# Splitting the output-weight load of a decode-attention kernel into 120 and 8 partitions

## The chip, the core and the metric

The kernel runs on one core of a Trainium2 chip. The metric is the device time of one execution in microseconds (us). Before the change the median of three runs is 2008.08 us (2006.43 to 2009.18).

## What is computed

Two independent attention blocks, A and B, decode one token each for a batch of two. Per block: 32 heads of 192, a cache of 8192 keys and values per head and batch entry, a model width of 640, everything in bf16. The two results are put side by side.

```python
q = (x @ wq).reshape(B, Sq, Hq, Dh).transpose(0, 2, 1, 3)      # B=2, Sq=1, D=640, Hq=32, Dh=192
scores = jnp.einsum("bhqd,bhkd->bhqk", q, k) * (Dh ** -0.5)    # k, v: (2, 32, 8192, 192)
p = _softmax(scores, axis=-1)
o = jnp.einsum("bhqk,bhkd->bhqd", p, v)
return o.transpose(0, 2, 1, 3).reshape(B, Sq, Hq * Dh) @ wo    # wo: (6144, 640)
# both blocks: jnp.concatenate([a, b], axis=-1)
```

Each key and value is used once, so the kernel is above all a stream of some 837 MB out of device memory.

## The kernel before

**Units.** The work is cut into 128 units, numbered `u`: block, then head, then batch entry. Head number `g` is `u // 2`. Each unit loads one 3 MB slab of keys (`kb`) and one of values (`vb`), laid out as 128 partitions by 64 rows by 192, so that each partition receives one run of 24576 bytes. There are two buffers for each.

**Engines.** VectorE multiplies the keys by the query, which stands broadcast over the partitions (L247 and L251), and sums a part of the products (L258, L262); ScalarE sums the other part (L269) and does the exponentials (L276); GpSimd does the maximum and the sum over partitions (L234, L238); TensorE multiplies the probabilities by the values (L344, 64 matmuls per unit). At the end of each pair of heads TensorE turns the result (L352) and multiplies it by the output weight (L379, called `f5` in the code, six matmuls), summing a block's result in `outps`.

**Weights.** Both weights are loaded in groups of four heads, numbered `w` from 0 to 15, with two buffers each: `wqs` (960 KB) and `wos` (960 KB). A load of `wos` has 128 partitions, and each partition receives two runs of 3840 bytes (three rows of the output weight for each of two head pairs).

**Order of the loads.** All loads are issued by SyncE (SP), one after the other, from one list written out by hand: keys of unit 0, keys of 1, values of 0, keys of 2, values of 1 and so on. `sp_wo(w)` stands behind the keys of unit `8w + 1`, ahead of the values of the unit before. A load waits until its buffer is free: keys for the multiply of two units ago (`d1b`), values for the matmuls of two units ago (`pv`), the output weight for the `f5` that last used its buffer. A DMA raises its semaphore by 16 when it has landed, and `reg` holds, for each name, the semaphore and the value that a reader waits for. Only the results (L320 of the code, `out_dram`, two rows of 640 bytes each) are stored from ScalarE's own queue.

**Who waits for the output weight.** `f5` of head pair `pp` waits for `("wo", (2 * pp) // HG)`. Waits are merged by `_Stream.emit`: an engine that has already waited for a value does not wait again, so there is one such wait on TensorE in each group, at the first `f5` that uses it.

## Time and profile before

| | |
|---|---|
| median of the runs | 2008.08 us (2006.43 to 2009.18) |
| profiled execution, first to last instruction (the span) | 2005.8 us |
| busy: TensorE, VectorE, ScalarE, GpSimd | 56%, 74%, 72%, 7% of the span |
| DMA packets | 55986, 838.05 MB, 418 GB/s in the mean |
| the load queue's packets | 98.8% of what 16 DMA engines have in the span |
| `wos` loads | 16 of 960 KB, 25.1 us from issue to landing (median) |

The profile gives the span of the one execution that was traced; it is 2.3 us below the median of the runs, which is what lies around the first and the last instruction and the scatter between executions. The page's DMA rows are means over 16 engines. A "landing" is the last of the 16 steps by which a load's semaphore rises. The trace also holds the time of every such step and of every DMA packet (start, duration, size, queue), but not the number of the engine that moved it.

### The profile page before, as it was taken

Reading aid. Unit: us, or ns where it says so; the run is one execution under the profiler, and the core shown is the slowest. Engines: PE = TensorE matmul, PEld = TensorE weight load, DVE = VectorE, ACT = ScalarE, POOL = GpSimd, SP = SyncE. Lnnn points to the kernel's source line nnn. Section 1 sums busy time; section 2 is a strip of 40 time slices with the busy share of each in tenths; the row PEclk is TensorE's granted clock in tenths of the full one; section 3 lists DMA queues with packets and bytes.
Section 4 is the critical chain, followed back from the end, with each engine's and each line's share of the span. In section 5 each row is a group of like instructions: output and inputs, shape, how many; then the busy total and the mean of one; then the engine's idle time right before and its main releaser. Section 6 shows DMA issues by size and latency. Waiting matters only on the chain.

```text
span 2005.8 us, 19822 instructions
## 1 busy us (share of the span) xinstructions
PE 1116.4 (56%) x5014; PEld 592.4 (30%) x5014; DVE 1484.8 (74%) x962; ACT 1435.5 (72%) x7811; POOL 143.6 (7%) x270
## 2 busy tenths in 40 slices
PE   2565555556555565556654565546655565555557
PEld 1232323223232233223322333223332233222323
DVE  7777877877777777777777767777677776877676
ACT  6776777767767676776767767777677776777776
POOL 2000100000000001000000000000000020000001
PEclk9776777777777777777777777777777777777778
DMA  9999999999999999999999999999999999999995
GB/s 389 429 428 431 430 429 431 429 431 427 428 426 426 423 413 430 419 425 420 420 430 407 424 420 418 429 411 428 416 417 433 413 423 422 410 433 414 430 417 235
DMA packets 55986, 838.05 MB, mean 418 GB/s; under 512 B 7352, under 2 KB 18240, under 8 KB 22848
## 3 DMA queue, kind: packets, MB, share of 16 engines
q1 hardware_dynamic: 55856, 836.79, 98.8%
q8 instruction: 39, 0.64, 0.1%
q14 instruction: 75, 0.61, 0.1%
q10 hardware_dynamic: 16, 0.01, 0.0%
HBM read 836.77 MB, written 0.01 MB: 417 GB/s over the span
## 4 chain that ended last, share of the span: by engine, by line
DMA 74%; PE 20%; DVE 4%; ACT 2%; issue 0%; POOL 0%; SPq 0%
DMA vb<-in_A_v_cache_dram 38%; DMA vb<-in_B_v_cache_dram 22%; PE ops L344 19%; DMA kb<-in_B_k_cache_dram 13%; DVE prodD L251 2%; DVE prodA L247 2%; ACT prodA L269 1%; DMA kb<-in_A_k_cache_dram 1%; POOL mg L234 0%; PE outps L379 0%; PE oTps L363 0%; PE oTps L352 0%; SPq L187 0%; SPq L194 0%; ACT pb L276 0%
## 5 line engine op out<-in xcount | busy, mean ns | idle before, releaser
L344 PE MATMUL ops<-vb,pb 128*33 128x384 bf16 x4096 | 954.1, 408 | 880.1 <-DMA vb<-in_A_v_cache_dram 451.2
L269 ACT ACTIVATE prodA<-prodA 128x192 bf16<-128x192 bf16 x3582 | 1239.7, 351 | 238.3 <-DVE prodA L247 238.2
L344 PEld LDWEIGHTS ops<-vb,pb 128*33 128x33 bf16 x4096 | 481.9, 120 | 1352.8 <-issue 1207.4
L269 ACT ACTIVATION_READ_ACCUMULATOR prodA<-prodA 128x1 f32 x3582 | 680.7, 190 | 0.0
L247 DVE TENSOR_TENSOR prodA<-kb,qbc 128x5376 bf16<-128x5376 bf16 x128 | 378.5, 2957 | 281.4 <-DMA kb<-in_A_k_cache_dram 142.5
L251 DVE TENSOR_TENSOR prodD<-kb,qbc 128x6912 bf16<-128x6912 bf16 x128 | 480.4, 3753 | 1.2 <-DMA kb<-in_A_k_cache_dram 1.2
L258 DVE TENSOR_TENSOR prodD<-prodD 128x3456 bf16<-128x3456 bf16 (+2 forms) x384 | 464.8, 1210 | 13.3
L254 DVE TENSOR_REDUCE mp<-sc 128x1 f32<-128x64 f32 x128 | 28.2, 220 | 201.4 <-ACT prodA L269 201.3
L234 POOL PARTITION_ALL_REDUCE mg<-mp x128 | 50.2, 392 | 1734.0 <-DVE mp L254 1734.0
L262 DVE TENSOR_REDUCE sc<-prodD 128x36 f32<-128x864 bf16 x128 | 134.8, 1053 | 4.4
L283 ACT ACTIVATE o_sb<-ops 1x384 f32<-1x384 f32 x63 | 30.3, 480 | 123.8 <-PE oTps L352 95.7
L311 ACT ACTIVATE qbc<-qps 128x384 bf16<-128x384 f32 x64 | 31.4, 491 | 92.5 <-PE qps L332 92.5
L273 ACT ACTIVATE nb<-mg 128x1 f32<-128x1 f32 x128 | 26.0, 203 | 99.5 <-POOL mg L234 99.5
L238 POOL PARTITION_ALL_REDUCE lall<-rs x128 | 85.8, 670 | 103.0 <-ACT pb L276 103.0
L352 PEld LDWEIGHTS oTps<-ones,o_sb 33*128 33x128 f32 x372 | 67.1, 257 | 9.8 <-issue 9.8
L352 PE MATMUL oTps<-ones,o_sb 33*128 33x1 f32 x372 | 69.8, 311 | 0.0
L276 ACT ACTIVATE pb<-sc,nb 128x64 bf16<-128x64 f32 x128 | 52.2, 408 | 4.3 <-ACT nb L273 0.2
L332 PE MATMUL qps<-wqs,xbc_0 128*128 128x384 bf16 x160 | 32.5, 335 | 6.1 <-DMA wqs<-in_A_wq_dram 6.1
L332 PE MATMUL qps<-wqs,xbc_1 128*128 128x384 bf16 x160 | 32.4, 334 | 0.6 <-ACT qbc L311 0.6
L379 PE MATMUL outps<-wos,oTz 128*4 128x320 bf16 x192 | 32.1, 304 | 0.1
L284 ACT ACTIVATE o_sb<-ops 1x384 f32<-1x384 f32 x63 | 30.4, 482 | 0.7
L276 ACT ACTIVATION_READ_ACCUMULATOR pb<-sc,nb 128x1 f32 x128 | 23.9, 187 | 0.0
(30 smaller groups left out, 84.8 us busy)
## 6 DMA issues: line engine op xcount, KB each, us to landing
vb<-in_A_v_cache_dram SPq DMA_DIRECT2D x64, 3072.0 KB, 23.0
kb<-in_A_k_cache_dram SPq DMA_DIRECT2D x63, 3072.0 KB, 24.0
kb<-in_B_k_cache_dram SPq DMA_DIRECT2D x63, 3072.0 KB, 23.8
vb<-in_B_v_cache_dram SPq DMA_DIRECT2D x62, 3072.0 KB, 23.2
wos<-in_A_wo_dram SPq DMA_DIRECT2D x8, 960.0 KB, 25.1
wqs<-in_B_wq_dram SPq DMA_DIRECT2D x8, 960.0 KB, 27.5
wos<-in_B_wo_dram SPq DMA_DIRECT2D x8, 960.0 KB, 25.1
wqs<-in_A_wq_dram SPq DMA_DIRECT2D x7, 960.0 KB, 27.5
```

The source lines that it names most:

```text
L234: return lambda eng: eng.partition_all_reduce(mg[u % 2][:], mp[u % 2][:], 128, bass.bass_isa.ReduceOp.max)
L238: return lambda eng: eng.partition_all_reduce(lall[g % 2][:, b:b + 1], rs[u % 2][:], 128, bass.bass_isa.ReduceOp.add)
L247: return lambda eng: eng.tensor_tensor(prodA[u % 2][:, 0:na, :], kb[u % NK][:, 0:na, :], qb_bc(u, na), ALU.mult)
L251: return lambda eng: eng.tensor_tensor(prodD[:, 0:T - na, :], kb[u % NK][:, na:T, :], qb_bc(u, T - na), ALU.mult)
L258: return lambda eng: eng.tensor_tensor(prodD[:, 0:nd, 0:w], prodD[:, 0:nd, 0:w], prodD[:, 0:nd, w:2 * w], ALU.add)
L262: return lambda eng: eng.tensor_reduce(sc[u % 2][:, na:T], prodD[:, 0:T - na, 0:24], AXL.X, ALU.add)
L269: return lambda eng: eng.activation(prodA[u % 2][:, t, :], prodA[u % 2][:, t, :], ACTF.Identity, accum_out=sc[u % 2][:, t:t + 1])
L276: return lambda eng: eng.activation(pb[u % 2][:, :, ::32], sc[u % 2][:].rearrange("p (j a) -> p j a", a=2), ACTF.Exp, bias=nb[u % 2][:], s ...
L332: ins = eng.matmul(qps[:, 0:QW], xbc[blk][b][:, c, :], wqs[w % 2][:, c, off:off + QW], start=(c == 0), stop=(c == DC - 1))
L344: ins = eng.matmul(ops[(u // B) % 2][0:33, b, 0:QW], pb[u % 2][:, j, :], vv[:, j, :], start=(j == 0), stop=(j == T // 2 - 1))
L352: ins = eng.matmul(oTps[:, 2 * i + b:2 * i + b + 1], o_sb[:, b, :, :].rearrange("p s (r i) -> p i (s r)", i=3)[:, i, :], ones33[:], start= ...
L379: ins = eng.matmul(outps[0:4, 0:NH2], oTz[pp % 2][:, i, 2 - 2 * half:6 - 2 * half], wos[w % 2][:, pr, i, half * NH2:(half + 1) * NH2], sta ...
```

## The change

Each load of `wos` is issued as two loads, one straight after the other: partitions 0 to 119 with the semaphore that was there, and partitions 120 to 127 with a new one (`wohsem`). `f5` waits for both. Sizes, order, buffers and all arithmetic stay as they are; SP issues 313 rows in place of 297.

```diff
+        wohsem = [sem(f"wohsem{i}") for i in range(2)]
...
             reg[("wo", w)] = (wosem[w % 2], 16 * (w // 2 + 1))
+            reg[("woh", w)] = (wohsem[w % 2], 16 * (w // 2 + 1))
...
-        def sp_wo(w):
+        WP = 120
+
+        def sp_wo(w, part):
             blk = (w * HG) // Hn
             h0 = (w * HG) % Hn
             src = blocks[blk]["wo"][h0 * Dh:(h0 + HG) * Dh, :].rearrange("(pr p i) n -> p pr (i n)", p=128, i=3)
-            return dma(wos[w % 2][:].rearrange("p pr i n -> p pr (i n)"), src, wosem[w % 2])
+            dst = wos[w % 2][:].rearrange("p pr i n -> p pr (i n)")
+            if part == 0:
+                return dma(dst[0:WP], src[0:WP], wosem[w % 2])
+            return dma(dst[WP:128], src[WP:128], wohsem[w % 2])
...
-            w = [("f4", pp), ("wo", (2 * pp) // HG), key("f5", pp - 1)]
+            w = [("f4", pp), ("wo", (2 * pp) // HG), ("woh", (2 * pp) // HG), key("f5", pp - 1)]
...
-                    S_sp.add(sp_wo(w), waits=[key("f5", ((w - 2) * HG + HG - 1) // 2 if w >= 2 else -1)])
+                    S_sp.add(sp_wo(w, 0), waits=[key("f5", ((w - 2) * HG + HG - 1) // 2 if w >= 2 else -1)])
+                    S_sp.add(sp_wo(w, 1))
```

## The prediction

> **What bounds the kernel now.** I read the page's sections 2 to 4 first, then the waits, the stages, and the tile `wos`.

> ```profile
> GB/s 389 429 428 431 430 429 431 429 431 427 428 426 426 423 413 430 419 425 420 420 430 407 424 420 418 429 411 428 416 417 433 413 423 422 410 433 414 430 417 235
> ...
> q1 hardware_dynamic: 55856, 836.79, 98.8%
> q8 instruction: 39, 0.64, 0.1%
> q14 instruction: 75, 0.61, 0.1%
> q10 hardware_dynamic: 16, 0.01, 0.0%
> ...
> DMA 74%; PE 20%; DVE 4%; ACT 2%; issue 0%; POOL 0%; SPq 0%
> ```

> The loads (q1) fill 98.8% of the mean DMA engine; 74% of the chain that ended last is DMA. No compute engine is over 74% busy. The waits, over all engines and then SP's own:

> ```profile
> PE ops L344 <- DMA vb<-in_A_v_cache_dram: 451.2, 64, 22.9
> PE ops L344 <- DMA vb<-in_B_v_cache_dram: 427.5, 64, 10.5
> ...
> SPq L187 <- PE ops L344: 1086.3, 126, 13.3
> SPq L187 <- DVE prodD L251: 777.8, 126, 12.0
> ```

> TensorE waits for values; SP waits for free buffers, its loads already queued. Two stages of the windows view (columns: length, then busy and count of PE, PEld, DVE, ACT, POOL, the clock, the DMA share, GB/s):

> ```profile
> 100.00:600.00 500.00, 282.97 (x1266) 150.18 (x1264) 371.33 (x242) 358.83 (x1956) 33.62 (x66) 0.73 1.01 429
> 600.00:1080.00 480.00, 269.60 (x1204) 143.42 (x1205) 358.34 (x232) 346.56 (x1889) 31.46 (x61) 0.73 1.00 422
> ```

> The same work runs at 429 GB/s up to 600 us and at 422 after, at one clock. The reason is in the 16 steps of each load's semaphore, one per DMA engine. From the trace's records, in us after the first step of the load:

> ```
> load ends at   2nd   8th   14th  15th  16th step
>  47 us (v)     0.03  0.15  0.35  0.36   0.84
> 207 us (k)     0.01  0.19  1.82  1.94   4.33
> 411 us (v)     0.03  1.67  2.03  2.25   9.17
> 571 us (k)     0.01  1.78  3.49  3.60  13.47
> 1317 us (k)    0.06  0.68  1.43  1.90  13.88
> ```

> **One DMA engine, call it X, falls behind all others** until it is some 13.5 us late. Then the two-deep buffers stop the rest, which is the fall to 422 GB/s. X never stops. Its landings between 23 and 1992 us add to 1981.2 us, against 1938.8 for its packets at their usual durations (a 24576-byte packet starts 912 ns after the one before). 64 of the 291 intervals are over 300 ns too long, by 46.9 us together; 62 of the 64 hold a q14 instruction packet. Such a packet of 8192 bytes sits in X's own sequence (309 ns, and the next takes some 380 ns longer: about 0.69 us). So X carries an instruction stream (by its even pace that of ScalarE with its 7811 instructions) besides its sixteenth of the loads, and X's sum is the kernel's time. The q8 packets fall on changing engines.

> **Which engine X is.** The stores of the result (q10) have two partitions each:

> ```profile
> out_dram<-out_sb ACTq DMA_DIRECT2D x4, 1.2 KB
> ```

> Their semaphore shows three steps per store, one at the issue and two later: two engines. At 1082.97 us one of the 640-byte packets starts where a packet of X ends, and at 1084.85 a q14 packet starts where the next of these ends. X is one of the two engines that even a two-partition DMA uses; both stores used the same two.

> **The change, part by part.** The old `wos` loads:

> ```profile
> L187 SPq DMA_DIRECT2D wos<-in_A_wo_dram x8: 435/436/2255, 11.3 to 870.2; - x8
> L187 SPq DMA_DIRECT2D wos<-in_B_wo_dram x8: 431/435/449, 993.8 to 1866.0; - x8
> ...
> DMA to landing us min/median/max: 14.3/25.1/25.3
> ```

> 1. Removed: 16 loads of 128 partitions. Each gives X 8 partitions, 16 packets of 3840 bytes; X spends 2.28 us on a load (mean of 16), so 142 ns a packet.

> 2. Added: 16 loads of 120 partitions. 128 went to 16 engines in equal parts and 2 to two, so I take 120 as 15 times 8, with X among the 15, since X is in the smallest set: 16 packets on X as before, no change in their number.

> 3. Added: 16 loads of 8 partitions, on 8 engines, X among them: two more packets on X per load, 2 x 0.142 = 0.285 us, and one more completion packet (they start 6 ns apart): 0.29 us, times 16 = **4.7 us**. X has no idle time, so all of it is on the path. The engine that is left out of the 15 saves 2.28 us per load, which buys nothing, as it already waits for X.

> [...]

> 4. Unknown: what a packet of such a split costs. Every load in this trace has 128 partitions, so each partition's bytes always came through one engine, and each engine ran alone at one rate (24576 bytes in 912 ns, 3840 in 142). With 15 engines that assignment has to shift, and X writes, at least for some partitions, where another engine writes all the time; others write where X does. If only the engine sets the pace, nothing is added: 4.7 us is the low end. If the destination does, two streams share it. Nearest row for that: from 1083 to 1088 us, as the results are stored and the stopped engines start again, packets of 24576 bytes take 1.0 to 2.1 us in place of 0.91, up to 2.3 times. At twice, X's 18 packets cost 18 x 2 x 0.142 - 2.28 = 2.85 us more per load, times 16 = **45.6 us**. If the others' packets also hold up X's keys and values for as long as a load's packets last, 2.28 more per load: 82 us, the high end. Below nothing this part has no way, as no packet here is faster than 912 ns or 142 ns.

> I take the middle, 45.6 us: the rate is the same to the nanosecond in all engines and for large and small packets, which looks like a fixed width that one stream fills; and I count only one of the two directions.

> [...]

> 5. SP issues 16 more DMAs, at the 0.44 us of the row above or less: 7 us on a queue that waited for buffers for 1864 us. Behind them stand the values of the unit before, issued some 15 us or more before they land. Without that cover they would cost 0.4 us per load. Nothing on the path.

> 6. TensorE waits 16 more times, before the first `f5` of a group. `wos` is issued at 248.3 us for a group whose `f5` is about five units of 15.7 us later; it lands after 25. Behind that wait are the next matmuls of L344, which wait for values anyway. Nothing, unless the load took over 70 us.

> Sum: 2005.8 + 45.6 = 2051.4 us of span; with the 2.3 us between span and median, **2053.7 us**.

> **The rivals.**

> - **Only the two packets count**: +4.7, 2012.8 us. For it: 4.7 is what the packet durations give alone, and they never vary with size. Against it: no row has two engines in one place. It is slower by just over 0.2%, which is about what a measurement of this kernel can tell from no change.
> - **X is the engine left out (faster).** If 120 partitions go to a set of 15 without X and the 8 to a set without it too, X saves 2.28 x 16 = 36.5 us. The next engine then sets the time. X's lag behind the 15th engine grew from 0.46 us at 23 us to 9.97 at 577.5, 17.2 ns per us, so 34 over the run; less 4.7 for the added packets: -29, 1979 us. It decides as soon as X's share falls by over 4.7 us in all. Against it: X carries packets of the two-partition stores, and a set of 15 without X next to a set of two with it would be odd. For it: the saving almost equals X's surplus.
> - **X's share stays** (8 of 120, none of the 8, no sharing of places): 2008.1 us.
> - **Fewer engines than 15**: if 120 goes in eights or less to a smaller set, X gets 15 or more partitions, at least 8 x 2 x 0.142 x 16 = +36 us, 2045 us, and over 2090 with sharing.

> **How the numbers follow.** Chances: places shared, with anything from +10 to +85 us, 0.55; two packets only, 0.22; X left out, 0.12; X's share unchanged, 0.05; fewer engines, 0.06. The range 2008 to 2090 holds the first two, the unchanged case and most of the last; below it lies X left out, above it a rest of 0.04. Faster by over 0.2%: 0.12. Within 0.2%: the unchanged case and a quarter of the two-packet one, whose 4.7 us is near the bound of 4.0: 0.10. Slower: 0.78.

> **What would show it.** X's time on a `wos` load (2.28 us between its landings) becomes about 2.57 if only packets count, and 4 to 7 us if places are shared; then also the durations of 3840-byte packets go from 149 ns towards 300, and packets of 24576 bytes near `wos` grow too. GB/s in the stage after 600 us falls below 422. One of the load's semaphores shows one early step (16 less 15), the other eight. I am wrong if X's lag shrinks and all engines land together (X left out), or if the wos packets still take 149 ns and the time rises by under 10 us.

## The result and the profile after

The changed kernel takes 2116.32 us (median of 4 runs, 2111.96 to 2117.5); the kernel before, in 4 runs, takes 2008.63. The ratio is 1.0536 (95% interval 1.0521 to 1.0551): slower by 107.7 us, where 45.6 were forecast, and above the end of the range, 2090.

The traced execution has a span of 2114.1 us, 108.3 more than before. First its page (sections 2 to 4):

```profile
GB/s 363 429 386 426 431 388 428 389 418 414 386 397 379 416 411 391 398 385 407 415 387 398 382 414 409 385 406 380 406 405 393 399 385 414 399 404 393 385 405 253
DMA packets 56099, 838.06 MB, mean 396 GB/s; under 512 B 7464, under 2 KB 18352, under 8 KB 22960
...
q1 hardware_dynamic: 55968, 836.79, 98.3%
...
DMA 78%; DVE 20%; ACT 1%; PE 0%; issue 0%; POOL 0%; SPq 0%
```

The same bytes, the DMA engines as full as before (98.3%), but 396 GB/s in place of 418. The row GB/s has holes of 379 to 390 all along; before, no slice between the first and the last was under 407. So packets are not waiting to be issued, they take longer. The q1 line has 112 packets more than before: 16 loads times (15 + 8 - 16) completion packets, so the two new loads use 15 and 8 engines; their semaphores show one early step and then 15 and 8 later ones.

The windows view, a stretch without and three with the first split load (columns: length, busy and count of PE, PEld, DVE, ACT, POOL, the clock, the DMA share, GB/s):

```profile
140.00:146.00 6.00, 2.40 (x8) 1.19 (x9) 5.90 (x4) 6.00 (x36) 0.00 (x0) 0.69 1.02 438
147.00:150.00 3.00, 3.00 (x13) 1.54 (x12) 0.83 (x2) 2.24 (x14) 0.35 (x1) 0.65 1.01 197
150.00:153.00 3.00, 1.64 (x11) 0.78 (x8) 0.00 (x0) 1.30 (x4) 0.39 (x1) 1.00 1.10 200
153.00:156.00 3.00, 0.00 (x0) 0.00 (x0) 0.57 (x1) 0.00 (x0) 0.00 (x0) 0.99 1.10 235
```

While `wos` is loaded, the DMA share is 1.01 to 1.10 and the core moves 197 to 235 GB/s, about half of the 438 before it. In the kernel before, with `wos` loaded among the keys and values in the same way, it ran at 425 and 451:

```profile
265.00:268.00 3.00, 3.00 (x13) 1.55 (x12) 2.90 (x4) 3.00 (x19) 0.00 (x0) 0.62 1.03 425
268.00:272.00 4.00, 2.96 (x19) 1.57 (x16) 1.03 (x3) 2.97 (x13) 0.74 (x2) 1.00 1.06 451
```

The tile `wos` (durations in ns, first and last start in us):

```profile
L189 SPq DMA_DIRECT2D wos<-in_A_wo_dram x16: 340/432/2327, 11.5 to 916.5; - x16
L189 SPq DMA_DIRECT2D wos<-in_B_wo_dram x16: 340/405/474, 1046.7 to 1968.6; - x16
...
DMA to landing us min/median/max: 17.9/31.8/32.8
```

`wos` lands 31.8 us after its issue (25.1 before). The waits (total us, times, longest), of all engines and then of SP's queue:

```profile
PE ops L351 <- DMA vb<-in_A_v_cache_dram: 507.3, 64, 26.9
PE ops L351 <- DMA vb<-in_B_v_cache_dram: 477.2, 63, 13.1
```

```profile
SPq L189 <- PE ops L351: 1182.1, 126, 15.0
SPq L189 <- DVE prodD L258: 784.3, 126, 13.2
```

The same waits as before are longer, none is new, and SP still waits for buffers. By size, from the trace's packet records (median ns of one): 3840 bytes, 149 before and 292 after; 24576 bytes, 912 in both, but 956 in the mean after and 925 before.

**Where the time went on X.** X, the engine that lands last in every load, never stops, so its landings can be laid end to end. Two kinds of interval changed. First, the one that holds `wos` (from the keys before it to the values after it), above the values' own 7.30 us. Second, the two loads just ahead of `wos`, above their own times: X is late (6.5 us behind the next engine at the third load, 9 to 13 us from the fifth on) and still writes these keys and values while the other engines already write `wos`. Means of 16, in us, with X's instruction packets in them in every kernel alike:

```
                          holds wos    two ahead    more per load, x 16     measured
before                       2.50         0.34               -                 -
after (120 + 8)              4.77         4.68      2.27 + 4.34 = 106        107.7
```

X pays 2.27 us as a guest, where its own `wos` packets go slowly, and 4.34 us as a host, where others' packets hold up its keys. In the load issued at 258.9 us its eight key packets, usually 912 ns, take 1199, 1634, 1813, 2533, 1640, 1016, 995 and 920; its 18 `wos` packets then take, in order:

```
149 149 149 169 302 314 314 314 304 301 185 171 284 301 301 300 | 286 296
```

(the last two are those of the 8-partition load). The other loads from the third on that could be followed packet by packet show the pattern of these 18 within some 40 ns a packet.

### The profile page after: what moved, and what is told of

The parts are those of the page before. It is cut to its first block, busy times and chain, and to the rows that moved or that the text cites. A ratio compares the mean times of both kernels' runs of the same rounds, so it can differ in the third digit from the quotient of the medians.

```text
span 2114.1 us, 19853 instructions
## 1 busy us (share of the span) xinstructions
PE 1119.0 (53%) x5014; PEld 592.8 (28%) x5014; DVE 1484.6 (70%) x962; ACT 1434.6 (68%) x7811; POOL 143.3 (7%) x270
## 3 DMA queue, kind: packets, MB, share of 16 engines
q1 hardware_dynamic: 55968, 836.79, 98.3%
## 4 chain that ended last, share of the span: by engine, by line
DMA 78%; DVE 20%; ACT 1%; PE 0%; issue 0%; POOL 0%; SPq 0%
DMA kb<-in_B_k_cache_dram 40%; DMA kb<-in_A_k_cache_dram 39%; DVE prodD L258 11%; DVE prodA L254 9%; ACT prodA L276 1%; PE ops L351 0%; POOL mg L241 0%; PE oTps L370 0%; PE outps L386 0%; SPq L189 0%; SPq L196 0%; ACT pb L283 0%; DVE mp L261 0%; ACT out_sb L322 0%; ACT nb L280 0%
## 5 line engine op out<-in xcount | busy, mean ns | idle before, releaser
L265 DVE TENSOR_TENSOR prodD<-prodD 128x3456 bf16<-128x3456 bf16 (+2 forms) x384 | 464.7, 1210 | 13.3
L269 DVE TENSOR_REDUCE sc<-prodD 128x36 f32<-128x864 bf16 x128 | 134.8, 1053 | 4.4
L339 PE MATMUL qps<-wqs,xbc 128*128 128x384 bf16 x320 | 64.8, 334 | 6.5 <-DMA wqs<-in_A_wq_dram 5.9
L339 PEld LDWEIGHTS qps<-wqs,xbc 128*128 128x128 bf16 x320 | 26.5, 99 | 29.6 <-issue 9.1
```

The source lines that it names most:

```text
L265: return lambda eng: eng.tensor_tensor(prodD[:, 0:nd, 0:w], prodD[:, 0:nd, 0:w], prodD[:, 0:nd, w:2 * w], ALU.add)
L269: return lambda eng: eng.tensor_reduce(sc[u % 2][:, na:T], prodD[:, 0:T - na, 0:24], AXL.X, ALU.add)
L339: ins = eng.matmul(qps[:, 0:QW], xbc[blk][b][:, c, :], wqs[w % 2][:, c, off:off + QW], start=(c == 0), stop=(c == DC - 1))
```

## The experiments

Two questions: what makes the split load dear, and is X late because instructions come through it? Theory P: a packet is slow where it goes to a place that another engine writes all the time. Rivals: a second DMA costs in itself (E); a load on 15 or 8 engines costs (K); the reading side costs (H).

**The second DMA and its wait, without a cut by partition.**

```diff
-            if part == 0:
-                return dma(dst[0:WP], src[0:WP], wosem[w % 2])
-            return dma(dst[WP:128], src[WP:128], wohsem[w % 2])
+            if part == 0:
+                return dma(dst[:, 0:1], src[:, 0:1], wosem[w % 2])
+            return dma(dst[:, 1:2], src[:, 1:2], wohsem[w % 2])
```

> The output weight is still loaded by two DMAs and waited for twice, but cut along the runs: each half has all 128 partitions and one of the two 3840-byte runs of each. Theory P (the cost is that engines write into places where another engine writes all the time, because the split moves partitions to other engines): no partition moves, so 2008 to 2011 us, wos packets at 149 ns. Rival E (a second DMA, its issue or its wait cost the time): 2080 to 2120 us. Rival K (what costs is a load on 15 or 8 engines in place of 16): 2008 to 2011 us.

2007.65 us, ratio 1.0001 (0.9992 to 1.001). Issue, wait and completion packets of a second load cost nothing that can be measured. E falls, and with it every cost on SP and TensorE:

```profile
L189 SPq DMA_DIRECT2D wos<-in_A_wo_dram x16: 431/433/2290, 11.4 to 871.5; - x16
L189 SPq DMA_DIRECT2D wos<-in_B_wo_dram x16: 432/436/462, 994.5 to 1867.1; - x16
...
DMA to landing us min/median/max: 12.3/24.4/25.3
```

As many issues as after, and landings as before.

**Cut at 112, both parts on all 16 engines.**

```diff
-        WP = 120
+        WP = 112
```

> The changed kernel with the cut at 112: both parts divide by 16, so by the count of engines each engine has 7 and 1 partitions, 8 in all as before, and no engine has more packets than before. Theory P: the partitions still come through other engines than in a load of 128, so 2070 to 2130 us and wos packets near 300 ns. Rival K (15 and 8 engines): 2008 to 2013 us, packets at 149 ns.

2086.89 us, ratio 1.0393 (1.0377 to 1.0408). No engine has more partitions than before or is left out (the semaphores have 16 steps each), and still it costs 79.4 us. K falls: it is not the number of engines. X pays 1.44 as a guest and 3.48 as a host, 79 us in 16 loads.

**The 8-partition load alone, beside a whole load.** The 8 partitions go to a spare tile.

```diff
+        wox = [sb(f"wox{i}", [128, HG // 2, 3, D], BF16) for i in range(2)]
...
             if part == 0:
-                return dma(dst[0:WP], src[0:WP], wosem[w % 2])
-            return dma(dst[WP:128], src[WP:128], wohsem[w % 2])
+                return dma(dst, src, wosem[w % 2])
+            return dma(wox[w % 2][:].rearrange("p pr i n -> p pr (i n)")[WP:128], src[WP:128], wohsem[w % 2])
```

> The whole load of 128 partitions as before, and after it the 8-partition load of the change, into a spare tile that nothing reads. It has the added load alone, with 8 engines and two more packets on the late engine. Theory P: the whole load costs nothing new; two packets at twice their length and some disturbance by the seven other engines: 16 x 0.3 to 16 x 1.0 us, 2013 to 2025 us. Rival K with the 8-engine load as the culprit: 2060 us or more.

2025.12 us, ratio 1.0086 (1.0071 to 1.0101): 17.7 us. X is the last of the eight engines, so it carries two more packets: 4.7 us by their usual length. The rest is disturbance; X pays 0.57 and 0.53 us more per load, 17.6 in all. The time is just above its expected range (2013 to 2025 us). If the costs of the two parts add up, most of the 107.7 us lies in the 120; no run has the 120 alone. Why 120 and 8 cost 28 us more than 112 and 16 is not shown either.

**Cut at 64.** The half that was expected of it is the author's guess, which no run had shown.

```diff
-        WP = 120
+        WP = 64
```

> The changed kernel with the cut at 64: 16 engines with 4 partitions each, twice. [...] So half of what the cut at 112 or 120 costs: X's first 8 packets at 149 ns, the other 8 near 300; 2040 to 2070 us. Rival A (any cut by partition costs the same): 2080 to 2120 us. Rival K (only counts of engines or packets matter): 2008 us.

2104.13 us, ratio 1.0472 (1.0454 to 1.0489): a miss. It costs 95.8 us, nearly as much as the cut at 120, and not half; that is what rival A had (any cut by partition costs the same). X's 16 packets in the load issued at 257.1 us:

```
149 149 149 187 322 327 301 295 | 282 299 188 176 302 315 324 305
```

Both halves slow down after a few packets. In the cuts at 120 and 64 the first four packets are quick (149 to 187 ns), and 11 and 12 again (171 to 188); the others take 282 to 327. In the cut at 112 the pattern stands two packets later (load issued at 255.7 us; the other loads from the third on are alike but for instruction packets):

```
149 149 149 149 149 176 311 325 309 292 301 296 178 178 | 306 316
```

There the first six are quick (149 to 176 ns) and 13 and 14 again (178). Why the quick ones stand where they do, and which partitions share a place, no run here shows.

**Eight loads of 16 partitions.**

```diff
-            if part == 0:
-                return dma(dst[0:WP], src[0:WP], wosem[w % 2])
-            return dma(dst[WP:128], src[WP:128], wohsem[w % 2])
+            return dma(dst[16 * j:16 * j + 16], src[16 * j:16 * j + 16], wosem[w % 2])    # j = 0..7
```

The loop over `j` and the count that `f5` waits for (128 a load in place of 16) are not shown.

> The output weight in eight loads of 16 partitions, one partition on each engine per load; X has its 8 partitions in all. [...] Rival E' (each further load costs by itself, 7 more in a group): linear in loads, but e1 already has it near zero.

2092.25 us, ratio 1.0418 (1.0403 to 1.0434): 84 us. One partition per engine in each load is no cure. X pays 1.20 us as a guest, less than in the other cuts; its packets take 149 to 276 ns in the load issued at 260.2 us, where each of the eight loads writes other partitions. As a host it pays 4.14.

**Which engine X is: loads of 17 partitions.** The whole load, and an extra one of 17 runs of 1920 bytes into a spare tile, from partition 4 in one kernel and from 8 in the other.

```diff
+        SX = 4        # 8 in the second kernel
...
+            return dma(wox[w % 2][SX:SX + 17, :], src[SX:SX + 17, 0, 0:960], wohsem[w % 2])
```

> The kernel before (whole load) plus one load of 17 partitions, 4 to 20, of 1920 bytes each per group, into a spare tile that nothing reads. [...]

> [...]

2014.24 us (1.003; 1.0019 to 1.0041) and 2011.42 us (1.0019; 1.001 to 1.0028). The semaphore shows one step at the issue and a single later one: one engine does it all. From the fifth load on it lands 4 to 11 us ahead of the `wos` load issued before it, so that engine is not X. At half the 142 ns of a 3840-byte packet, its 17 packets would take that engine 1.2 us, some 19 us in 16 loads, an estimate; 6.0 and 3.1 us show in the times. X is in the sets of two and of eight but not of one. By the later steps of their semaphores the loads here ran on 16 engines for 128, 112, 64 and 16 partitions, 15 for 120, 8 for 8, 2 for 2 and 1 for 17. Which of the 16 X is by number, no run shows. The two medians differ by 2.8 us, but the intervals overlap, so this pair does not show that it matters to X which partitions the other engine writes.

**Destination or source: one row read by all.** A whole load, and an extra load of 3840 bytes per partition into a spare tile, all read from the same row: 120 partitions in one kernel, 128 in the other.

```diff
+        NX = 120      # 128 in the second kernel
...
+            return dma(wox[w % 2][0:NX, :], src[0:1, 0, :].broadcast_to([NX, 3 * D]), wohsem[w % 2])
```

> The kernel before (whole output weight) plus one load per group into 120 partitions of a spare tile that nothing reads, 3840 bytes each, all read from the same row. Where it is read from is then the same for all engines and all partitions; only the destination is cut. By bytes alone X has 8 more packets: 16 x 8 x 0.142 = 18 us, 2026 us. Theory P (destination): about half of what the cut at 120 costs on top, 2055 to 2090 us, packets of X up to 300 ns. Rival H (the cost is on the reading side, rows of the weight read by other engines): the same as the next run.

> As the one before with 128 partitions: same row, same bytes per engine on the 15, one engine more. All theories: by bytes, 2022 to 2032 us, packets at 149 ns. If reading one row by all engines is slow in itself, it shows here too.

2074.23 us (1.032; 1.0303 to 1.0337) and 2025.45 us (1.0082; 1.0067 to 1.0097). With 128 the extra bytes cost 17.5 us, about what their packets take (8 x 16 x 0.142 = 18 us). With 120, with the same bytes on X and one row as the source of everything, 48.8 us more. H falls. X's eight extra packets, in the loads issued at 250.9 and 255.5 us:

```
128 partitions:  149 149 149 149 149 149 149 149
120 partitions:  149 149 149 149 282 328 193 184
```

X pays 0.87 us as a guest (4.62 against 3.75 in the interval) and 2.03 as a host (2.38 against 0.35), about half of what the change costs, for half of its bytes: 46 us in 16 loads.

**Is X late because of instructions?** The kernel before, with fewer of ScalarE's 3582 small sums at L269; VectorE sums those rows in its place. The loads are untouched.

```diff
-    NA_MAIN = min(cfg.get("NA", 28), T - 2)
-    NA_LAST = min(cfg.get("NA_LAST", 26), T - 2)
+    NA_MAIN = min(cfg.get("NA", 20), T - 2)         # 14 and 10 in the two others
+    NA_LAST = min(cfg.get("NA_LAST", 20), T - 2)    # 14 and 10
```

> The kernel before, with ScalarE summing 20 of the 64 rows of products per unit in place of 28 (26 in the last) and VectorE the other 44; nothing in the loads changes. Theory X (the late engine is late because ScalarE's instructions come through it): some 2000 fewer ScalarE instructions, 16 fewer instruction packets there at 0.73 us each: 12 us less, 1994 to 1999 us. Rival S (that engine is slow in itself): 2006 to 2010 us. Rival V (VectorE, with 1.0 us more in a unit of 15.7, becomes late): over 2010 us.

> The kernel before with ScalarE summing 14 of 64 rows. Theory X: against the 20 rows of the earlier run another 12 instruction packets less on X, 9 us less: 1984 to 1990 us. Rival V (VectorE now late): over 1996 us.

> The same with 10 rows. Theory X: another 8 packets less, 6 us: 1978 to 1985 us, as far as X is still the last engine (the 15th was 34 us better over the whole run). VectorE is at 14 of 15.5 us per unit by the durations of before; if that is too much, 1990 us or more.

1995.23 us (0.9937; 0.992 to 0.9953), 1988.02 us (0.9897; 0.9882 to 0.9911) and 1983.46 us (0.9875; 0.986 to 0.989). The instruction packets on q14 number 75, 59, 47 and 39, and the time falls by 12.2, 7.2 and 4.6 us: 0.76, 0.60 and 0.57 us for each packet less. X's lag behind the next engine near 570 us is 9.2 us before, then 5.7, 3.6 and 2.3. X's surplus is ScalarE's instructions. Rival S falls, and V too, with VectorE at 88%:

```profile
span 1981.5 us, 15218 instructions
## 1 busy us (share of the span) xinstructions
PE 1110.6 (56%) x5014; PEld 590.6 (30%) x5014; DVE 1743.6 (88%) x962; ACT 634.9 (32%) x3207; POOL 166.1 (8%) x270
...
GB/s 389 430 427 430 432 427 433 431 427 432 428 430 430 431 429 429 432 430 429 430 429 431 430 430 428 431 428 430 429 425 433 424 432 431 425 429 426 429 428 210
```

The row GB/s, which fell to 407 to 423 in places before, now stays at 424 to 433 between the first slice and the last: X no longer stops the others as early. This version, without the change, beats both kernels by 1.25% and 6.3%.

**All cuts in one table**, with the working of the table above (the last line against the whole load with 128):

```
                     guest   host   (g + h) x 16   measured
112 + 16              1.44   3.48        79           79.4
64 + 64               1.88   4.17        97           95.8
8 x 16                1.20   4.14        85           84.0
whole + 8             0.57   0.53        18           17.7
one row to 120        0.87   2.03        46           48.8
```

The two terms account for every kernel's time within 2.5 us.

## Why the prediction was right and wrong

- **What bounds the kernel** was right, and the runs with fewer ScalarE instructions show it: one DMA engine sets the time, and what is taken from it comes off the total (0.57 to 0.76 us for each instruction packet less).
- **Steps 1 and 2** were right: 15 engines, X among them, which no run had shown before. X's being left out, its unchanged share, and fewer than 15 engines are ruled out: the semaphore has one early step and 15 later ones, and X's 16 packets are there.
- **Step 3**, two more packets on X, is right in kind: the semaphore of the 8 partitions has eight later steps, which no run had shown before, and X carries two packets of that load; its 4.7 us are part of the 17.7 that the 8-partition load costs alone. The rival in which only they count is ruled out.
- **Step 4 was mis-sized, and this is the term that failed.** The cause that it names, places shared by two engines, is the one that the runs left standing, and packets went from 149 ns to about 300, the doubling that was taken. X's own packets cost 2.27 us more per load with the two added ones in it; the step had 2.85, a little too much, as the first four and two later ones stay quick (149 to 185 ns). But I counted one of the two directions. The other, X as the host, was put at nothing in the forecast and at 2.28 us in the high end, "as long as a load's packets last". It is 4.34 us, twice X's own loss: 69 of the 106 us. The 2.28 was no bound. It assumed that the others' packets pass at full speed through X's place; but those are slow themselves (292 ns in the median of all 3840-byte packets, 149 before): the core falls to 197 to 235 GB/s for the 9 us from 147 to 156, and X's keys take up to 2533 ns in place of 912. That X's loss comes to 4.34, and not more or less, is not derived; why others cost X as a host twice what X pays as a guest stays open.
- **The chances** use a +85 us that no run shows; step 4's own high end is 82. In its place the runs showed 107.7 us for the change and 79.4 to 95.8 for the other cuts of the whole tile.
- **Three readings of the trace** were inexact. The 1981.2 us run from X's landing at 14.7 us to that at 1995.9, not from 23 to 1992. In the row of 1317 us the 14th and 15th steps stand at 1.90 and 2.80 us. And packets did not run at one rate: 939 of the 32256 packets of 24576 bytes took over 1000 ns before the change, up to 2688, some behind an instruction packet and many in bursts after 550 us. None of the three changes which step failed.
- **Steps 5 and 6**, SP and TensorE at nothing, were right: the run with two full halves has the same issues and waits and no loss.
- **What would show it** came as told: `wos` packets towards 300 ns, key packets near `wos` longer, the GB/s lower, one early step and eight. The forecast of slower held; the range, which took the high end as the end, did not.

## What to carry to other kernels

When loads set the time, look at the 16 steps of a load's semaphore one by one: if one engine is always last and never stops, as here, its own sum is the time, and a mean share of 98.8% hides that. In loads of 128 partitions the 3840-byte packets stayed at 149 ns (median); cut such a load along each partition's bytes if it must be cut (nothing lost here, ratio 1.0001), and not by partition in a stream as full as this (1% for an added load of 8 partitions, 4 to 5% for the cuts of the whole tile). And count what instructions cost: some 4600 fewer on ScalarE gave 24.5 us, though ScalarE was never the bound.
